# A Strassen-form feed-forward kernel: the sum S1 formed wholly by VectorE, and one small sum of product P5 queued behind an add of product P1

## The chip, the core and the metric

The kernel runs on one core of a Trainium2 chip. The metric is the device time of one execution in microseconds (us). Engines are named as in the profile: PE (TensorE matmul), PEld (its weight loads), DVE (VectorE), ACT (ScalarE), POOL (GpSimd), SP (SyncE, which here only issues DMAs).

## The reference

A causal convolution of 7 taps along the sequence, one set of softmaxed taps per head, followed by a two-layer feed-forward network with a hard-swish between the layers:

```python
# x (8, 4096, 192), weight (8, 7), w_in (192, 2048), w_out (2048, 192)
w = softmax(weight, axis=-1)
y[b, s, d] = sum_k w[head(d), k] * x_padded[b, s + k, d]     # 6 zeros ahead of each sequence
h = y.reshape(32768, 192) @ w_in
g = h * clip(h + 3, 0, 6) / 6
out = g @ w_out                                              # (32768, 192)
```

Everything is float32.

## The kernel before

**Blocks.** The 32,768 tokens go in 32 blocks of 1,024 tokens, each as two halves of N = 512. Block 0 has a path of its own. Blocks 1 to 31 each run `first_layer` and then `second_layer`. While one block is in these, DVE and ACT also form the convolution of the block after the next one.

**First layer.** The 2,048 hidden columns are 16 units of 128 x 1,024 (both token halves). A unit is 18 matmuls on PE (L438) into one of four PSUM slots, a relu on ACT (L312) and a gate multiplication on DVE (L316) that writes the result g to SBUF. A unit's slot comes free with its gate.

**Second layer.** The product g @ w_out is done in Strassen's form (Winograd's variant): g is taken as a 2 x 2 matrix of parts A11, A12, A21, A22, each of 8 chunks of 128 x 512, and seven products P1 to P7 of sums of parts replace eight. The sums needed from g are S3 = A11 - A21, S1 = A21 + A22, S2 = S1 - A11 and S4 = A12 - S2. S1 overwrites A21, S2 overwrites A11. S3 is formed towards the end of the first layer, two chunks at a time (`g_sums`, L386), three times on POOL and the last time on DVE. S1 is formed in place:

- chunks 0 to 3 by a DMA that adds (`onto`, L481, called at L513): source A22, destination A21, with `accum_op=add`, issued from POOL's queue after unit 11;
- chunks 4 to 7 by two DVE adds of 128 x 1,024 (`add`, L406, called at L515), after unit 15.

**Level two.** Output columns come in groups of 32 (q = 0, 1, 2). For the third group, products P1, P4 and P5 are themselves done in Strassen's form, with *small sums* of quarter parts of their left operand (`small_sums`, L535) and products of 128 x 256 (`small`). For P5 the operand is S1, and its small sums lie in A22's memory (`s5 = A22`): sum 1 = x21 + x22, sum 3 = x11 - x21, sum 2 = sum 1 - x11, sum 4 = x12 - sum 2. They are formed on DVE by `sum_s5`. P1's small sums are formed earlier, on POOL. P4's are gathered by adding DMAs into a tile `z` and two further tiles (L481, `z<-g` and `z<-z`), the last of them issued at L516, after the S1 adds.

**Order.** The order of the second layer is written by hand. Four streams (three column groups, and one for level two) each have a clock that counts *ticks*; a 128 x 512 matmul costs two ticks and a 128 x 256 matmul one, and the four streams use four column groups of the array at the same time. All streams end at tick 81 (45 by the assert at L691, then 2 x 8 + 2 x 2 + 2 x 8). `do(t, ...)` enters other work at t - 0.5; everything is sorted by its time and issued in that order, and each engine works through its own share in that order.

Of stream 3, the steps of `level_two(1, ...)` matter here: 4 chunks and a half of plain product until tick 9, then the small products in the order 1, 5, 6, 2, 7, 3, 4, of four ticks each. So small product 7 of P1 is at ticks 25 to 29, 3 at 29 to 33, and 4 at 33 to 37. After 7 and after 3, DVE adds a result into `p1` (L721 and L722, which the profile shows under L406 as `p<-psum,p 32x256`). These are called *add 7* and *add 3* below. Product 4 accumulates onto the same PSUM place C that add 7 reads, so PE waits at tick 33 until add 7 is done. `level_two(5, ...)` follows from tick 37: product 1 reads S1 itself, product 5 (tick 41) sum 1, product 6 (tick 45) sum 2.

The lines that put P5's small sums into this order:

```python
        for t, n in ((15.5, 1), (15.5, 3), (28.5, 2)):   # L754
            do(t, sum_s5, n)
```

Sums 1 and 3 are entered at 15.0, sum 2 at 28.0, add 7 at 28.5, add 3 at 32.5. Sum 1 overwrites a part of A22 that product P4 reads until tick 15, sum 2 one that it reads until tick 28.

Of the kernel before, what the change touches and what calls it, by code (L numbers as in the profile page):

```python
# [31 lines left out]
def kernel(  # L32
# [28 lines left out]
    NP = NC // 2  # L61
# [61 lines left out]
    def own_tiles(name):  # L123
        return [yo.tile([P, K3, N], F32, name=f"{name}{n}", tag=f"y{n}") for n in range(2)]
# [179 lines left out]
    A11, A21, A12, A22 = (g4[:, :, j] for j in range(4))  # L304
    S2, S1, S4 = A11, A21, A12
# [5 lines left out]
    def relu(r6, h):  # L311
        nc.scalar.activation(r6, h, ACT.Relu, bias=half[:], scale=1.0 / 6.0)  # L312

    def gate(g_, h):

        nc.vector.scalar_tensor_tensor(  # L316
            out=g_, in0=g_, scalar=1.0, in1=h, op0=ALU.min, op1=ALU.mult
        )
# [57 lines left out]
    def g_sums(engine, which, slots, width):  # L376

        forms = {
            3: (S3, A11, A21, ALU.subtract),
            2: (S2, S1, A11, ALU.subtract), 4: (S3, A12, S2, ALU.subtract),  # L380
        }
        for n in which:
            o, a, b, op = forms[n]
            for p in slots[::width]:
                r = slice(p, p + width)
                engine.tensor_tensor(out=o[:, r], in0=a[:, r], in1=b[:, r], op=op)  # L386
# [18 lines left out]
    def add(out, x, y, op=ALU.add):  # L405
        nc.vector.tensor_tensor(out=out, in0=x, in1=y, op=op)  # L406
# [25 lines left out]
    def products(n, slot, s, steps=range(3), begin=False, end=False):  # L432
        group, c = divmod(n, NP)
        for m_ in steps:
            wn, yn = PASSES[m_]
            for k in range(2):
                r = slice(k * D2, (k + 1) * D2)
                nc.tensor.matmul(  # L438
                    out=psum[:, 2 * slot + k], lhsT=r32(w_in_parts[wn][r, c, s]),
                    rhs=r32(y_other[r, yn, s] if group else y_own[yn][r, s]),  # L440
                    start=begin and m_ == 0, stop=end and m_ == 2, skip_group_check=True,
                )

    def places(n, slot):
        group, c = divmod(n, NP)
        return g4[:, c, 1:3] if group else g4[:, c, 0::3], psum[:, 2 * slot : 2 * slot + 2]


    def sums_a22():

        z2, z4 = (
            part[:].rearrange("p s n -> p (s n)")[:, : NP * TH // 2]
            .rearrange("p (u t) -> p u t", t=TH)
            for part in z_early
        )
        return z[:, :, 1], z2, z[:, :, 0], z4

    def first_layer(i, jobs):

        def unit(n):  # L460
            slot = free_slots.pop(0)
            for m_ in range(3):
                for s in range(K3):
                    products(n, slot, s, (m_,), s == 0, s == K3 - 1)
            to, both = places(n, slot)
            relu(to, both)
            gate(to, both)
            free_slots.append(slot)

        count = 2 * NP  # L470
        x11, x12, x21, x22 = four_parts(A22)

        def begin_sums():
            z_early[:] = own_tiles("z")
            seed(sums_a22()[1], x11, -1.0)

        def seed(to, x, sign):
            nc.scalar.mul(to, x, sign)  # L478

        def onto(to, x):  # L480
            nc.gpsimd.dma_start(out=to, in_=x, accum_op=ALU.add)  # L481


        def z13(u0, u1):
            onto(z[:, u0:u1].rearrange("p u c t -> p (u c) t"), A22[:, 2 * u0 : 2 * u1, halves[1]])

        hu = NP // 4
        s4_sums = {
            hu + 1: [lambda: seed(z[:, :hu, 0], x11[:, :hu], -1.0)],
            hu + 2: [lambda: seed(z[:, :hu, 1], x21[:, :hu], 1.0), lambda: z13(0, hu)],  # L490
            NP - 1: [lambda: seed(z[:, hu:, 0], x11[:, hu:], -1.0)],
            NP: [lambda: seed(z[:, hu:, 1], x21[:, hu:], 1.0), lambda: z13(hu, 2 * hu)],
            NP + 1: [begin_sums],
            NP + 2: [lambda: seed(sums_a22()[3], x12, -1.0)],
        }
        for job in jobs.get(-1, ()):
            job()
        for n in range(count):
            unit(n)
            for job in jobs.get(n, ()):  # L500
                job()
            for job in s4_sums.get(n, ()):
                job()
            if n == 1:
                s1.append(ot.tile([P, NP, N], F32, name="s1", tag="shared")[:])
            if n < NP and n % 2:
                small_sums(s1[-1], A11, (1, 2, 3, 4), nc.gpsimd, every[n - 1 : n + 1])
            if n > NP and n % 2:
                pair = slice(n - NP - 1, n - NP + 1)
                g_sums(nc.gpsimd if n + 1 < count else nc.vector, (3,), range(NP)[pair], 2)  # L510
                if n == NP + 3:
                    onto(sums_a22()[1], z[:, :, 1])
                    onto(S1[:, : NP // 2], A22[:, : NP // 2])  # L513
        for pair in (slice(NP - 2, NP), slice(NP - 4, NP - 2)):
            add(S1[:, pair], A21[:, pair], A22[:, pair])  # L515
        onto(sums_a22()[3], sums_a22()[1])  # L516

# [3 lines left out]
    def four_parts(x):  # L521
        return [x[:, c::2, t] for t in halves for c in range(2)]

    def small_sums(to, x, which, engine=nc.gpsimd, r=every):

        r = slice(r[0], r[-1] + 1)
        x11, x12, x21, x22 = four_parts(x[:, r])
        s1, s2, s3, s4 = four_parts(to[:, r])
        forms = {
            1: (s1, x21, x22, ALU.add), 2: (s2, s1, x11, ALU.subtract),  # L530
            3: (s3, x11, x21, ALU.subtract), 4: (s4, x12, s2, ALU.subtract),
        }
        for n in which:
            o, p, q, op = forms[n]
            engine.tensor_tensor(out=o, in0=p, in1=q, op=op)  # L535
# [13 lines left out]
    def second_layer(i, between):  # L549
        last = i + 1 == NB  # L550
        ours = [free_slots.pop(0) for _ in range(3)]
        d, e, b, c, a, x_ = (psum[:, 2 * n + k] for n in ours for k in range(2))
# [16 lines left out]
        def do(t, fn, *args, **kw):  # L569
            streams[3].append((t - 0.5, lambda: fn(*args, **kw)))  # L570
# [180 lines left out]
                s2 = four_parts(s5)[1]  # L751
                add(z[:, :, 0], four_parts(S1)[1], s2, ALU.subtract)

        for t, n in ((15.5, 1), (15.5, 3), (28.5, 2)):  # L754
            do(t, sum_s5, n)
        do(31, tiles)
        do(37, copy, out=b[m], in_=p1[:])
# [78 lines left out]
    with tc.manual_schedule():  # L836
# [101 lines left out]
        for r in range(2 * NP):  # L938
# [12 lines left out]
            n = joins.get(r)  # L951
# [72 lines left out]
        for i in range(1, NB):  # L1024
            rest = conv[2 if i > 1 else 3 :]
            jobs = {4 * n + 1: [job] for n, job in enumerate(rest[1:])}
            jobs[-1] = left + rest[:1]
            first_layer(i, jobs)
            conv = []

            def begin_conv():
                x_tiles[i + 2] = load_x(i + 2)
                conv.extend(conv_jobs(i + 2))

            between = []
            if i + 1 < NB:
                between = [(43.6, split_high), (62, split_rest), (63, swap_parts)]
            if i + 2 < NB:
                between += [(20, begin_conv), (64, lambda: conv[0]()), (72, lambda: conv[1]())]
            left = second_layer(i, between)  # L1040
# [33 lines left out]
```

## Time and profile before

| | us |
|---|---|
| median of 3 runs | 2235.2 (2234.88 to 2235.53) |
| the profiled execution | 2235.09 |
| its span in the profile | 2233.3 |
| PE busy | 2222.2 (100% of the span) |
| DVE busy | 1828.4 (82%) |
| ACT busy | 1159.6 (52%) |
| POOL busy | 893.9 (40%) |

The span is the time from the first to the last instruction that the profile records. The profiled execution's own time is 1.8 us more. Busy time of PE is modelled from pipelined matmuls, so 100% does not say that PE never paused. The granted PE clock is full in all forty slices.

### The profile page before, as it was taken

How to read it: one execution, taken by the hardware profiler on the slowest of the kernel's cores; microseconds unless marked ns; L12 is line 12 of the kernel's file. 1: busy time of each engine (PE TensorE's matmuls, PEld its weight loads, DVE VectorE, ACT ScalarE, POOL GpSimd, SP SyncE). 2: the span in 40 equal slices, each digit the busy share in tenths (PEclk: the TensorE clock that was granted, in tenths of full speed). 3: DMA queues.
4: the chain of work that ended last, by engine and by line, in shares of the span. 5: the costliest groups of instructions: out<-in, count | busy, mean ns of one | idle time of the engine just before them, and what ended most of it. 6: DMA issues, size and time to landing. Idle time of an engine off the chain costs nothing.

```text
span 2233.3 us, 51856 instructions
## 1 busy us (share of the span) xinstructions
PE 2222.2 (100%) x22466; PEld 1519.3 (68%) x22466; DVE 1828.4 (82%) x1650; ACT 1159.6 (52%) x1607; POOL 893.9 (40%) x803
## 2 busy tenths in 40 slices
PE   9999999999999999999999999999999999999998
PEld 5577767667766676766676666776677666677676
DVE  8877888878888778887888878888878888788876
ACT  7455554455554555545555445554455554555544
POOL 4534442244522445323454224542245432454423
PEclk9999999999999999999999999999999999999999
DMA  7355544545545555345553554544545545555344
GB/s 164 67 106 92 100 72 96 105 86 100 89 81 103 98 90 103 72 96 106 94 100 65 101 104 89 100 76 91 105 86 100 88 85 99 99 93 104 68 88 66
DMA packets 302180, 208.09 MB, mean 93 GB/s; under 512 B 208608, under 2 KB 261344, under 8 KB 301952
## 3 DMA queue, kind: packets, MB, share of 16 engines
q0 software_dynamic: 70320, 98.65, 27.8%
q1 hardware_dynamic: 230392, 105.86, 21.9%
q8 instruction: 176, 2.88, 0.5%
q10 hardware_dynamic: 1240, 0.27, 0.1%
q14 instruction: 52, 0.43, 0.1%
HBM read 31.72 MB, written 25.17 MB: 25 GB/s over the span
## 4 chain that ended last, share of the span: by engine, by line
PE 92%; DVE 2%; POOL 2%; DMA 2%; issue 1%; ACT 1%; SPq 0%; DVEq 0%; POOLq 0%; ACTq 0%
PE psum L573 47%; PE psum L438 44%; PE psum L327 2%; DMA g<-g 1%; POOL s L535 1%; DMA out_dram<-results 0%; DVE g L535 0%; POOL s L386 0%; DVE s L386 0%; POOL z L481 0%; DVE p L406 0%; DMA x<-in_x_dram 0%; DVE results L406 0%; SPq L353 0%; DVE g L316 0%
## 5 line engine op out<-in xcount | busy, mean ns | idle before, releaser
L573 PE MATMUL psum<-g,w_out 128*32 128x512 f32 (+1 forms) x6092 | 1055.8, 531 | 0.0
L312 ACT ACTIVATE g<-psum,half 128x1024 f32<-128x1024 f32 x512 | 570.3, 1116 | 319.7 <-PE psum L438 303.6
L535 POOL TENSOR_TENSOR s<-g 128x256 f32<-128x256 f32 x248 | 245.2, 989 | 1214.4 <-DVE g L316 928.0
L316 DVE SCALAR_TENSOR_TENSOR g<-g,psum 128x1024 f32<-128x1024 f32 x512 | 616.2, 1216 | 129.2 <-ACT g L312 128.7
L573 PE MATMUL psum<-s,w_out 128*32 128x256 f32 (+1 forms) x3272 | 631.7, 570 | 0.1
L438 PE MATMUL psum<-y,w_in 64*128 64x512 f32 x4608 | 534.9, 388 | 0.3
L438 PE MATMUL psum<-y_other,w_in 64*128 64x512 f32 x4608 | 529.0, 386 | 0.1
L438 PEld LDWEIGHTS psum<-y,w_in 64*128 64x128 f32 x4608 | 428.5, 184 | 121.5 <-issue 26.0
L573 PEld LDWEIGHTS psum<-g,w_out 128*32 128x32 f32 x6092 | 385.6, 109 | 168.6 <-issue 47.2
L438 PEld LDWEIGHTS psum<-y_other,w_in 64*128 64x128 f32 x4608 | 431.6, 184 | 91.1 <-DMA y_other<-y 0.5
L927 DVE SCALAR_TENSOR_TENSOR y<-x,c_sb,y 128x1536 f32<-128x1536 f32 x186 | 335.8, 1806 | 1.9 <-ACT y L925 1.8
L573 PE MATMUL psum<-g,w_s 128*32 128x256 f32 x1488 | 327.7, 379 | 3.2 <-DVE p L406 2.9
L386 POOL TENSOR_TENSOR s<-g 128x1024 f32<-128x1024 f32 x93 | 303.2, 3260 | 5.5 <-DVE g L316 4.8
L573 PEld LDWEIGHTS psum<-s,w_out 128*32 128x32 f32 x3272 | 223.9, 110 | 103.8 <-issue 69.3
L535 DVE TENSOR_TENSOR g<-g 128x1024 f32<-128x1024 f32 x93 | 108.7, 1220 | 152.7 <-DMA g<-g 113.3
L573 PEld LDWEIGHTS psum<-g,w_s 128*32 128x32 f32 x1488 | 154.8, 110 | 109.9 <-DVE p L406 23.4
L573 PE MATMUL psum<-z,w_s 128*32 128x256 f32 x992 | 206.3, 380 | 0.0
L386 DVE TENSOR_TENSOR s<-g 128x2048 f32<-128x2048 f32 (+1 forms) x93 | 179.9, 1934 | 1.5
L478 ACT ACTIVATE z<-g 128x512 f32<-128x512 f32 x186 | 143.0, 769 | 56.1 <-DVE g L316 54.4
L573 PE MATMUL psum<-s,w_s 128*32 128x256 f32 x744 | 170.7, 379 | 0.0
L570 ACT COPY psum<-psum 32x512 f32<-32x512 f32 (+1 forms) x217 | 106.3, 490 | 108.7 <-PE psum L573 103.9
L925 ACT ACTIVATE y<-x,c_sb 128x1536 f32<-128x1536 f32 x31 | 48.9, 1578 | 211.3 <-issue 211.3
(97 smaller groups left out, 1726.3 us busy)
## 6 DMA issues: line engine op xcount, KB each, us to landing
y_other<-y SPq DMA_DIRECT2D x124, 384.0 KB, 5.0
z<-g POOLq DMA_DIRECT2D x62, 512.0 KB, 5.4
z<-z POOLq DMA_DIRECT2D x62, 512.0 KB, 7.3
g<-g POOLq DMA_DIRECT2D x31, 1024.0 KB, 13.3
out_dram<-results SPq DMA_DIRECT2D x378, 64.0 KB, 2.0
x<-in_x_dram SPq DMA_DIRECT2D x53, 388.5 KB, 11.5
g<-in_moe_w_in_dram SPq DMA_DIRECT2D x16, 192.0 KB, 5.6
stage<-in_moe_w_out_dram SPq DMA_DIRECT2D x8, 384.0 KB, 5.2
```

The source lines that it names most:

```text
L312: nc.scalar.activation(r6, h, ACT.Relu, bias=half[:], scale=1.0 / 6.0)
L316: nc.vector.scalar_tensor_tensor(out=g_, in0=g_, scalar=1.0, in1=h, op0=ALU.min, op1=ALU.mult)
L327: lambda p=p: nc.tensor.matmul(out=bank[j * QS : (j + 1) * QS, tokens], lhsT=w_out[:, p, w, cols], rhs=x[:, p, tokens], start=(first and p ...
L386: engine.tensor_tensor(out=o[:, r], in0=a[:, r], in1=b[:, r], op=op)
L438: nc.tensor.matmul(out=psum[:, 2 * slot + k], lhsT=r32(w_in_parts[wn][r, c, s]), rhs=r32(y_other[r, yn, s] if group else y_own[yn][r, s]), ...
L478: nc.scalar.mul(to, x, sign)
L535: engine.tensor_tensor(out=o, in0=p, in1=q, op=op)
L570: streams[3].append((t - 0.5, lambda: fn(*args, **kw)))
L573: nc.tensor.matmul(out=out, lhsT=w, rhs=x, start=start, stop=True, tile_position=(0, j * QS), skip_group_check=True,)
L925: jobs = [lambda: nc.scalar.mul(y[:], x[:, :, 0:N], c_sb[:, 0:1])]
L927: jobs.append(lambda k=k: nc.vector.scalar_tensor_tensor(out=y[:], in0=x[:, :, k : k + N], scalar=c_sb[:, k : k + 1], in1=y[:], op0=ALU.mu ...
```

## The change

S1 is formed by four DVE adds of two chunks each, in the order of chunks 6-7, 4-5, 2-3, 0-1. The adding DMA for chunks 0 to 3 is gone. P5's small sum 2 is entered at 28.7 instead of 28.0, that is, behind add 7 (28.5) instead of ahead of it, and still ahead of add 3 (32.5). The order of instructions on PE, ACT and SP is the same as before; on POOL one DMA issue per block is gone; on DVE there are two more adds per block, and sum 2 and add 7 have changed places.

```diff
@@ -510,8 +510,8 @@
                 g_sums(nc.gpsimd if n + 1 < count else nc.vector, (3,), range(NP)[pair], 2)
                 if n == NP + 3:
                     onto(sums_a22()[1], z[:, :, 1])
-                    onto(S1[:, : NP // 2], A22[:, : NP // 2])
-        for pair in (slice(NP - 2, NP), slice(NP - 4, NP - 2)):
+        for c in range(NP - 2, -1, -2):
+            pair = slice(c, c + 2)
             add(S1[:, pair], A21[:, pair], A22[:, pair])
         onto(sums_a22()[3], sums_a22()[1])
 
@@ -751,7 +751,7 @@
-        for t, n in ((15.5, 1), (15.5, 3), (28.5, 2)):
+        for t, n in ((15.5, 1), (15.5, 3), (29.2, 2)):
             do(t, sum_s5, n)
```

## The prediction

> **What bounds the kernel now.** I read the page first: PE is busy for 2222.2 of 2233.3 us and the chain that ended last is 92% PE, so only time in which PE stands still can be won. The chain in order of time shows where it does (start, length, what; L438 is the first layer, L573 the second):
>
> ```profile
> 94.84 32.86 PE psum L438 x288
> 127.71 35.04 PE psum L573 x252
> 162.75 32.87 PE psum L438 x288
> ...
> 437.24 32.87 PE psum L438 x288
> 470.11 13.04 PE psum L573 x85
> 483.20 0.54 issue
> 483.81 1.16 issue
> 485.45 20.87 PE psum L573 x142
> 506.32 32.87 PE psum L438 x288
> ...
> 2124.04 35.04 PE psum L573 x255
> 2159.08 32.87 PE psum L438 x288
> ```
>
> Every first layer takes 32.9 us. The second layer takes 35.04 in blocks 1 and 30, which is 81 ticks of 0.433 us with nothing left over. In block 6 (from 470.11) it takes 36.21: the chain leaves PE at 483.2 and comes back at 485.45. From there to the end it is 20.87, so in a block of 35.04 PE gets to that place 35.04 - 20.87 = 14.17 us after its start; in block 6 at 15.34, 1.17 late. The two lists of waits say who is waited for (engine, line, releaser: total us, times, longest):
>
> ```profile
> DVE g L535 <- DMA g<-g: 113.3, 24, 5.8
> PEld psum L573 <- DVE p L406: 23.4, 28, 1.6
> ```
>
> PE waits in 28 blocks for an add into p1, and DVE ahead of that for the adding DMA of S1 (g<-g). DVE's timeline in block 6 shows the two linked (start, length, last the idle time before it):
>
> ```profile
> 473.82 2.36 DVE L406 TENSOR_TENSOR g<-g 128x1024 f32<-128x1024 f32 x2
> 481.44 3.51 DVE L535 TENSOR_TENSOR g<-g 128x1024 f32<-128x1024 f32 x3 [5.25 <-PE psum L573]
> 484.97 0.96 DVE L406 TENSOR_TENSOR p<-psum,p 32x256 f32<-32x256 f32 x2
> ```
>
> The S1 adds end at 476.18. DVE idles 5.25 us, runs sums 1, 3 and 2, then adds 7 and 3. The row names PE as releaser, but sum 1 needs of PE only ticks up to 15 (6.5 us after the start, 476.6); the DMA, issued at 467.59, is what remains, about 13.7 us to landing in this block (481.3). PE's product 4 waits for add 7, behind the three sums. Block 1 is the same work with an early DMA:
>
> ```profile
> 131.41 2.36 DVE L406 TENSOR_TENSOR g<-g 128x1024 f32<-128x1024 f32 x2
> 135.76 2.36 DVE L535 TENSOR_TENSOR g<-g 128x1024 f32<-128x1024 f32 x2 [1.99 <-DMA g<-g]
> 139.89 1.23 DVE L535 TENSOR_TENSOR g<-g 128x1024 f32<-128x1024 f32 x1 [1.77 <-PE psum L573]
> 141.15 0.43 DVE L406 TENSOR_TENSOR p<-psum,p 32x256 f32<-32x256 f32 x1
> 142.15 0.43 DVE L406 TENSOR_TENSOR p<-psum,p 32x256 f32<-32x256 f32 x1 [0.58 <-PE psum L573]
> ```
>
> Here add 7 ends at 141.58, which is 13.87 after the start 127.71 and 0.30 ahead of the 14.17 at which PE wants it: no pause.
>
> **The DMA taken out.** All the pause goes if nothing else is late at tick 33. Its size comes from the chain: the first layers of blocks 1 and 31 start at 94.84 and 2159.08, 2064.24 apart, 30 periods. A period without pause is 67.91 (94.84 to 162.75; block 30's is 67.92). 30 x 67.91 = 2037.30, so all pauses are 26.94 us. Adding up each second layer's excess over 35.04 gives 26.85, in blocks 2 to 29 alone, from 0.47 to 1.71 each. I take 26.9.
>
> POOL loses an issue of 1.79 us per block. That is worth nothing: the next POOL instruction, S3's sum of chunks 4-5, starts at 468.54 in block 6, just after the gate it needs (467.23 + 1.22 = 468.45). The other accumulating DMAs and the x loads get their megabyte of company less; no wait of PE on them is in the lists, so this counts as zero too. Were POOL's queue to hold P4's last DMA back, the cover is long: it is issued at 473.05, lands about 8.7 later (481.8), and PE reads it at tick 39, 470.11 + 16.9 = 487.0.
>
> **Two adds put in.** The row above has two adds of the same shape in 2.36 us, 1.18 each, so 2.36 per block on DVE and 73 us over 31 blocks, all in the place where DVE idled for the DMA. In times after the second layer's start (block 6): adds end at 6.07 + 2.36 = 8.43; sums 1 and 3 (2.36) end at 10.8. In block 1 add 3 starts at 14.44 after waiting for PE; add 7's product is four ticks (1.73) earlier, so add 7 can start at 12.71. DVE is therefore 1.9 us early, against 0.3 late to 1.7 late before. Bounds for an add whose price at this place no row shows: 1.18 by the rows above, and 2.41 by the same shape on POOL. At 2.41 the adds end at 10.9, the sums at 13.3, add 7 at 13.7, still ahead of 14.17. The point from which it costs PE is (14.17 - 0.43 - 2.36 - 6.07) / 2 = 2.65 per add. I take 1.18, since it is the same engine, shape and neighbours (the two adds ran beside DMAs in every block at the same 2.36). A price below zero has no source.
>
> **Sum 2 behind add 7.** Add 7 runs 12.71 to 13.14, sum 2 (1.23) 13.17 to 14.40, and add 3 starts at 14.44 as in block 1. Queued behind sum 2 on DVE are add 3 and the S2 sums; the first is not moved, by 0.04 us. If it were late by a few tenths nothing follows: the next write to what it reads is at tick 45 (19.5), which is also when PE first wants sum 2. This edit and the DMA's removal overlap: with the DMA gone, sum 2 ahead of add 7 would give block 1's 13.87, no pause either. It is worth 0 in the sum; alone, with the DMA kept, it would take up to 1.2 off each pause. It turns a margin of 0.30 into 1.03.
>
> **The sum.** The profiled execution took 2235.09 (span 2233.3 and 1.8 around it). 2235.09 - 26.9 = 2208.2. The median of the runs is 0.11 more, 2235.2: I predict 2208.3.
>
> **Rivals.**
> *Part of the pause stays.* Something besides the DMA is late at add 7, say an adding DMA that sum 3 also waits for (z<-g, whose reading of A22 must end). For it: sums wait for several semaphores, and the row in block 6 names the wrong one. Against: blocks 1, 30 and 31 have all these and no pause. If the smallest pause, 0.47, stays in 28 blocks, 13 us come back: 2221; a tenth of a us each gives 2211.
>
> *No gain: the first layer takes it back.* If DVE with 73 us more work set the pace, PE would pause in the first layer instead and the time stay near 2235. Against: in block 2, straight behind the pause-free block 1, the first layer takes 32.87 as everywhere, and everything DVE does after add 3 is timed by PE's own progress.
>
> *Slower: POOL gets ahead of the convolution.* POOL's S3 sum takes 3.9 us in block 6, 2.41 where no convolution step of DVE runs:
>
> ```profile
> 464.45 2.41 POOL L386 TENSOR_TENSOR s<-g 128x1024 f32<-128x1024 f32 x1 [0.16 <-DVE g L316]
> 467.59 1.78 POOL L481 DMA_DIRECT2D g<-g  x1
> 468.54 3.90 POOL L386 TENSOR_TENSOR s<-g 128x1024 f32<-128x1024 f32 x1
> ```
>
> DVE's convolution step (L927, two SBUF inputs) runs 468.37 to 470.18 there; 3.90 - 2.41 = 1.49 is about what of it was left when POOL began. So one of the two waits the other out, and the one that starts first wins. The removed issue stands right ahead of this POOL instruction. If POOL now started ahead of 468.37, DVE's step and the two gates behind it would come 2.4 us later, and PE, which wants the slot of gate 14 at tick 3, would pause 2.4 in 28 blocks: 2208 + 67 = 2275. Against: the POOL sum starts 0.09 after the gate it needs, and the convolution step 0.08 before that gate's end, so the order is set by the gate and not by the issue. It decides only from a shift of 0.17.
>
> The Trainium skill ("SBUF — State Buffer", "Who interferes with whom") states the same as a rule that speaks against this change: a DVE instruction with two SBUF inputs and a POOL instruction that reads SBUF exclude each other for their whole length. By that rule each new S1 add could hold up POOL, or be held up; by it alone the sum would gain up to 2.41 per block if POOL had work there. The trace agrees with the rule at L927, by the 1.49 above, and shows POOL without an SBUF-reading instruction from 472.44 in block 6 until the next block's first sums, so here it would add 0.
>
> **How the numbers follow.** Forecast 0.87 (2206.8 to 2209.8: the runs' spread of 0.3, and 0.04 per block either way, half the scatter of the first layers, which take 32.86 to 32.93); part of the pause stays 0.07; no gain 0.02; slower 0.04. The range, 2206.8 to 2212, is the forecast and the nearer part of the second case. About 0.2% (4.5 us) is what a measurement of this kernel can tell from no change. Faster takes the first two, 0.94; same 0.02; slower 0.04.
>
> **What would show it.** Right: second layers of 35.04 in all blocks, no row of PEld waiting for DVE p L406 of any size, four S1 adds of 4.7 us in a row, sums 1 and 3 straight behind them without idling, DVE idle about 1.9 us ahead of add 7. Wrong: a pause at tick 33 or a new one at ticks 3, 41 or 45, first layers above 32.9, or S1 adds well over 1.18.

## The result and the profile after

The changed kernel takes 2210.2 us (median of 4 runs, 2209.9 to 2210.5), against 2235.3 for the kernel before (median of 4). The ratio is 0.9888, 95% interval 0.9871 to 0.9905. The prediction was 2208.3, in the range 2206.8 to 2212.0. The time is in the range, the pauses went as forecast, and 1.9 us of the gain did not come.

The profiled execution took 2210.5, its span is 2208.7. The chain of the changed kernel in order of time (start, length, what), blocks 2 and 3:

```profile
162.91 32.87 PE psum L438 x288
195.78 26.47 PE psum L573 x183
...
231.60 4.07 DMA out_dram<-results
...
235.79 0.71 DVE results L412
236.50 1.70 DVE y L927
238.20 1.14 DVE g L316
...
239.39 24.78 PE psum L438 x216
264.16 35.04 PE psum L573 x256
```

and around block 6:

```profile
468.07 35.04 PE psum L573 x253
503.11 32.90 PE psum L438 x288
536.01 35.04 PE psum L573 x254
```

Every second layer of blocks 1 to 30 is now 35.04. The row of PEld waiting for DVE p L406 (23.4 us before) is gone from the list of waits. What is new is in the first piece: after block 2 the chain leaves PE, goes over a store to DRAM of 4.07 us and a DVE transpose (L412), and comes back to PE in the first layer of block 3.

DVE's timeline of block 6 (start 468.07), which answers to the one of block 6 before:

```profile
471.78 4.63 DVE L406 TENSOR_TENSOR g<-g 128x1024 f32<-128x1024 f32 x4
476.51 2.36 DVE L535 TENSOR_TENSOR g<-g 128x1024 f32<-128x1024 f32 x2
478.82 0.07 DVE L87 MEMSET x<- 64x18 f32 x1
481.20 0.43 DVE L406 TENSOR_TENSOR p<-psum,p 32x256 f32<-32x256 f32 x1 [2.31 <-PE psum L573]
481.66 1.23 DVE L535 TENSOR_TENSOR g<-g 128x1024 f32<-128x1024 f32 x1
482.92 0.96 DVE L406 TENSOR_TENSOR p<-psum,p 32x256 f32<-32x256 f32 x2
```

Four S1 adds in 4.63, sums 1 and 3 right behind, then DVE waits 2.31 for PE before add 7, which ends at 481.63, 0.6 ahead of the 482.24 (468.07 + 14.17) at which PE wants it.

The books of the two profiled spans, 2233.3 and 2208.7, 24.6 apart: pauses in second layers 26.85 before and 0.08 after (-26.8); first layers above 32.865, added up over blocks 2 to 31, 0.24 before and 1.67 after (+1.4), of it 0.47, 0.17, 0.39 and 0.41 in blocks 3, 5, 11 and 13; the stretch ahead of block 1 +0.2, the stretch from the last second layer's start to the end of the span 41.42 before and 42.00 after (+0.6). That last one is 41.2 to 41.8 in the kernels e1 to e5 and e8 below, which change little there, so I take it as scatter of single executions.

### The profile page after: what moved, and what is told of

Its sections match the earlier page's. It is cut to its first block, busy times and chain, and to the rows that moved or that the text cites. A ratio compares the mean times of both kernels' runs of the same rounds, so it can differ in the third digit from the quotient of the medians.

```text
span 2208.7 us, 51797 instructions
## 1 busy us (share of the span) xinstructions
PE 2199.7 (100%) x22466; PEld 1588.0 (72%) x22466; DVE 1898.5 (86%) x1712; ACT 1158.0 (52%) x1607; POOL 866.6 (39%) x772
## 3 DMA queue, kind: packets, MB, share of 16 engines
q1 hardware_dynamic: 230392, 105.86, 23.4%
## 4 chain that ended last, share of the span: by engine, by line
PE 96%; DVE 2%; DMA 1%; ACT 1%; SPq 0%; POOL 0%; issue 0%; DVEq 0%
PE psum L573 48%; PE psum L438 46%; PE psum L327 2%; DMA out_dram<-results 1%; DVE s L386 0%; DVE results L406 0%; SPq L353 0%; PE psum L851 0%; PE psum L859 0%; DVE y L927 0%; DVE results L412 0%; DVE y L424 0%; ACT g L312 0%; DVE g L316 0%; DMA y_other<-y 0%
## 5 line engine op out<-in xcount | busy, mean ns | idle before, releaser
L573 PE MATMUL psum<-g,w_out 128*32 128x512 f32 (+1 forms) x6092 | 1041.5, 531 | 0.0
L573 PE MATMUL psum<-s,w_out 128*32 128x256 f32 (+1 forms) x3272 | 623.9, 570 | 0.1
L573 PEld LDWEIGHTS psum<-g,w_out 128*32 128x32 f32 x6092 | 395.7, 110 | 145.3 <-issue 38.3
L573 PE MATMUL psum<-g,w_s 128*32 128x256 f32 x1488 | 316.9, 379 | 0.0
L386 POOL TENSOR_TENSOR s<-g 128x1024 f32<-128x1024 f32 x93 | 296.9, 3192 | 14.3 <-DVE g L316 13.3
L573 PEld LDWEIGHTS psum<-s,w_out 128*32 128x32 f32 x3272 | 196.8, 110 | 100.2 <-issue 78.0
L573 PE MATMUL psum<-z,w_s 128*32 128x256 f32 x992 | 201.3, 379 | 0.0
L406 DVE TENSOR_TENSOR p<-psum,p 32x256 f32<-32x256 f32 (+1 forms) x155 | 73.7, 476 | 96.5 <-PE psum L573 91.4
```

The lines of the kernel that those rows point to most:

```text
L573: nc.tensor.matmul(out=out, lhsT=w, rhs=x, start=start, stop=True, tile_position=(0, j * QS), skip_group_check=True,)
```

## The experiments

### Which half of the change carries the gain

**No DMA, old order (e1).** S1 wholly by DVE, sum 2 ahead of add 7 as before:

```diff
-        for t, n in ((15.5, 1), (15.5, 3), (29.2, 2)):
+        for t, n in ((15.5, 1), (15.5, 3), (28.5, 2)):
```

> S1 wholly by DVE as in the change, but sum 2 ahead of add 7 as before. Theory (the pause is the adding DMA's landing, and sum 2's place is worth nothing once the DMA is gone): second layers of 35.04 us in all blocks with add 7 ending some 0.3 ahead of PE, time 2210.2 within 1. Rival (sum 2 ahead of add 7 is what makes PE wait): each block keeps its smallest pause of about 0.47, 31 x 0.47 = 15, time about 2225.

Measured 2209.9 (2209.5 to 2210.2), ratio to before 0.9888 (0.9874 to 0.9903), as the changed kernel. All second layers 35.04. Its DVE timeline in block 6 (start 467.71 by the first matmul of the second layer):

```profile
479.89 1.22 DVE L535 TENSOR_TENSOR g<-g 128x1024 f32<-128x1024 f32 x1 [1.36 <-PE psum L573]
481.15 0.43 DVE L406 TENSOR_TENSOR p<-psum,p 32x256 f32<-32x256 f32 x1
```

Add 7 ends at 481.58, 13.87 after the start, as in block 1 before. The theory holds, the rival is out by 15 us: with the DMA gone, the place of sum 2 is worth nothing.

**The DMA kept, new order (e2).**

```diff
-        for t, n in ((15.5, 1), (15.5, 3), (28.5, 2)):
+        for t, n in ((15.5, 1), (15.5, 3), (29.2, 2)):
```

> The adding DMA kept, only sum 2 moved behind add 7. Theory: PE then waits for DMA landing + sums 1 and 3 (2.36) + add 7 (0.43), which is 1.2 less than before, so of the pauses of before only what exceeds some 1.2 stays, about 2.2 us over all blocks; the first layers lose what they lose in the changed kernel; time 2211 to 2213. Rival (the DMA's removal carries the gain and the order is worth nothing): 2235.

Measured 2214.0 (2213.4 to 2215.3), ratio 0.9908 (0.9891 to 0.9924). That is 1 us above what I expected, and far from the rival's 2235. Its block 2 (start 195.6) shows the rest of a pause:

```profile
199.35 2.36 DVE L406 TENSOR_TENSOR g<-g 128x1024 f32<-128x1024 f32 x2
207.40 2.36 DVE L535 TENSOR_TENSOR g<-g 128x1024 f32<-128x1024 f32 x2 [5.69 <-DMA g<-g]
209.71 0.07 DVE L87 MEMSET x<- 64x18 f32 x1
209.81 0.43 DVE L406 TENSOR_TENSOR p<-psum,p 32x256 f32<-32x256 f32 x1
```

Here the wait is put down to the DMA itself. Add 7 still comes behind it, but one sum sooner. The second layers are 3.5 us above 35.04 in all (2.2 expected; sums 1 and 3 started as late as 12.01 into the layer here, 11.93 before), the first layers 2.6. So the two halves of the change are two cures for one pause: either alone removes 23 to 27 us of the pauses at tick 33, and they do not add.

### Why the DMA was late

**x loads issued later (e4).** The kernel before, with

```diff
-                x_tiles[i + 2] = load_x(i + 2)
+                x_tiles[i + 2] = load_x(i + 2, nc.scalar)
...
-                between += [(20, begin_conv), (64, lambda: conv[0]()), (72, lambda: conv[1]())]
+                between += [(30, begin_conv), (64, lambda: conv[0]()), (72, lambda: conv[1]())]
```

> The kernel before, adding DMA and order of sum 2 kept, but the two loads of x issued from ACT's queue at tick 30 instead of from SP at the second layer's start, so that they run after the adding DMA. Theory (the DMA is late because it shares the DMA engines with the x loads; alone it lands as early as in blocks 1, 30 and 31): sums 1 and 3 start 8 to 9 us into the second layer instead of 10.7 to 11.9, no pauses, time 2209 to 2212. Rival (the DMA is late by itself, or queued behind P4's DMAs): starts stay near 11, time 2235.

Measured 2211.4 (2211.1 to 2211.6), ratio 0.9895 (0.9880 to 0.9909). Issues and times to landing, before and here (line queue, count, KB each, median us):

```profile
g<-g POOLq DMA_DIRECT2D x31, 1024.0 KB, 13.3
x<-in_x_dram SPq DMA_DIRECT2D x53, 388.5 KB, 11.5
```

```profile
g<-g POOLq DMA_DIRECT2D x31, 1024.0 KB, 11.0
x<-in_x_dram ACTq DMA_DIRECT2D x51, 388.5 KB, 5.7
```

Apart, both land sooner, by 2.3 and 5.8 us. Sums 1 and 3 start 8.1 to 10.3 us into the second layer (8 to 9 expected), and but for 0.07 us in one block there is no pause, with the adding DMA and the old order in place. The edit moves the loads to another time and to another queue at once. That the time is what counts is seen in the kernel before: blocks 1, 30 and 31, whose second layers issue no loads, have the adding DMA land 10.5, 10.5 and 11.1 us after its issue, from the same queues, against 12.8 to 14.2 in the others. And in the changed kernel, where the loads stay on SP at the old place and the adding DMA is gone, they land in 6.0 (median). So the DMA was not too slow as such: it ran into the loads of x.

### What two more adds on DVE cost

**Two and four further instructions (e5, e6).** The changed kernel with `k` = 2 or 4 maxima of an S1 pair with itself:

```diff
             add(S1[:, pair], A21[:, pair], A22[:, pair])
+            if c < 2 * k:
+                add(S1[:, pair], S1[:, pair], S1[:, pair], ALU.max)
```

> The changed kernel with two further DVE instructions of an S1 add's shape per block (the maximum of an S1 pair with itself, in place), right behind the first two chunk pairs formed. It prices the adds: the place holds as if each of the two new adds cost 2.36 us. Theory (DVE has 1.9 us or more to spare ahead of add 7, and the price from which PE waits is 2.65 per new add): sums 1 and 3 end at about 13.1 us into the second layer, add 7 still starts when PE lets it (13.2), no pause, time 2210.2 within 1. Rival (DVE has no such slack; every us more on it shows): 31 x 2.36 = 73, time 2283.

> The same with four further DVE instructions per block (4.72 us). Theory: sums 1 and 3 end at about 15.5, add 7 at 15.95, PE goes on at 16.0 instead of 14.24, a pause of 1.77 in 31 blocks, 55 us; behind the pause DVE stands 0.4 earlier against PE's end than without it, as in the kernel before, so that first layers are 32.87 again (1.5 back); time about 2264. Rival (DVE has no slack): 31 x 4.72 = 146, time 2356.

In e5 the two maxima stand behind the last two pairs formed (chunks 2-3 and 0-1) and not the first two; the work ahead of sum 1 is the same. Measured with two: 2209.4 (2209.2 to 2210.9), ratio 0.9887 (0.9872 to 0.9902), no change. With four: 2276.5 (2275.9 to 2276.9), ratio 1.0185 (1.0168 to 1.0202). Block 6 of each, two first (second layers start at 467.7 and 478.2):

```profile
471.42 7.15 DVE L406 TENSOR_TENSOR g<-g 128x1024 f32<-128x1024 f32 x6
478.68 2.36 DVE L537 TENSOR_TENSOR g<-g 128x1024 f32<-128x1024 f32 x2
480.98 0.07 DVE L87 MEMSET x<- 64x18 f32 x1
481.08 0.43 DVE L406 TENSOR_TENSOR p<-psum,p 32x256 f32<-32x256 f32 x1
```

```profile
481.88 9.67 DVE L406 TENSOR_TENSOR g<-g 128x1024 f32<-128x1024 f32 x8
491.66 2.36 DVE L537 TENSOR_TENSOR g<-g 128x1024 f32<-128x1024 f32 x2
493.96 0.07 DVE L87 MEMSET x<- 64x18 f32 x1
494.07 0.43 DVE L406 TENSOR_TENSOR p<-psum,p 32x256 f32<-32x256 f32 x1
```

With two, the S1 work is 2.52 longer and add 7 goes only 0.2 later. DVE's idle time ahead of it is used up, and add 7 ends 13.8 into the layer, 0.4 ahead of the 14.17 at which PE wants it. With four it is 5.04 longer and every second layer is 37.2, a pause of 2.19 each, 65.6 over blocks 1 to 30. I expected a pause of 1.77 and a time of about 2264. Of the 0.42 between the pauses, 0.32 is in the S1 work: 5.04 longer and not 4.72. The rival's 2283 and 2356 are out. Of the 5.04, then, 2.85 were free (5.04 less 2.19). With the 1.16 that each new add takes by itself (4.63 / 4), that is 1.16 + 2.85 / 2, some 2.6 us for each of the two, as the prediction had it and about twice their price.

### Where the missing 1.9 us went

**Four store buffers (e3).** The fourth transpose of a block writes into the buffer of its first, so it waits until that one is stored. The changed kernel with a fourth buffer:

```diff
-        xts[:] = range(3, 6)
+        xts[:] = [NP - 1, *range(3, 6)]
...
-            if last:
-                xts.insert(0, NP - 1)
```

> The changed kernel with four instead of three transposed-result buffers in every block, so that the fourth transpose of a block does not wait for the store of its first. Theory (the 1.9 us that the prediction missed are first layers of 33.0 to 33.3 in blocks 3, 5, 11 and 13, where the fourth transpose waited up to 2 us for a store and the first gate came later than about 6.87 us into the layer): all first layers 32.87, time 2208.5 to 2209.2. Rival (the two more DVE adds, or DVE's busier second layer, make the gates late): no change, 2210.2.

Measured 2208.2 (2208.0 to 2208.4), ratio to before 0.9881 (0.9866 to 0.9895): the fastest of all, 0.3 below the range that I gave and 1.7 below e1, which ran beside it and takes the time of the changed kernel. All first layers are 32.87, all second layers 35.04. The place in block 3, DVE's timeline before, after and here (the first layer starts at 231.51, 230.82 and 230.69):

```profile
235.75 0.71 DVE L412 STREAM_TRANSPOSE results<-results 96x512 f32<-96x512 f32 x1 [1.59 <-DMA out_dram<-results]
236.39 1.77 DVE L927 SCALAR_TENSOR_TENSOR y<-x,c_sb,y 128x1536 f32<-128x1536 f32 x1
238.08 2.34 DVE L316 SCALAR_TENSOR_TENSOR g<-g,psum 128x1024 f32<-128x1024 f32 x2
```

```profile
235.79 0.71 DVE L412 STREAM_TRANSPOSE results<-results 96x512 f32<-96x512 f32 x1 [1.96 <-DMA out_dram<-results]
236.43 1.77 DVE L927 SCALAR_TENSOR_TENSOR y<-x,c_sb,y 128x1536 f32<-128x1536 f32 x1
238.12 2.34 DVE L316 SCALAR_TENSOR_TENSOR g<-g,psum 128x1024 f32<-128x1024 f32 x2
```

```profile
233.73 0.71 DVE L412 STREAM_TRANSPOSE results<-results 96x512 f32<-96x512 f32 x1
234.37 1.77 DVE L925 SCALAR_TENSOR_TENSOR y<-x,c_sb,y 128x1536 f32<-128x1536 f32 x1
236.06 2.34 DVE L316 SCALAR_TENSOR_TENSOR g<-g,psum 128x1024 f32<-128x1024 f32 x2
```

The wait for the store was there before, 1.59 us, and the first gates came 6.57 into the layer with no harm (32.89). After the change they come at 7.30, and the layer is 33.34. Over the blocks, a layer is longer by what the first gate comes later than about 6.8. So the stores are one part. The other is that DVE reaches the end of a second layer 0.40 us later against PE: the second of its four transposes starts 1.24 to 1.29 us before the next first layer (its first weight load) in the changed kernel and in block 1 of the kernel before, and 1.68 us before it in the 28 blocks where the kernel before had paused at tick 33. In e6, with a pause at tick 33 in every block, it is 1.64 to 1.66 again and no first layer is above 32.89. A pause at tick 33 of 0.40 us or more hands DVE 0.40 us, and the change takes that back.

**Four store buffers, nothing else (e8).** The same edit in the kernel before.

> The kernel before with four instead of three transposed-result buffers, and nothing else. Theory (with the pause at tick 33 DVE stands 0.4 us earlier against PE's end, so the waits for the stores stay just short of delaying PE): first layers were 32.87 already, all pauses at tick 33 stay, time 2234.7 to 2235.3. Rival (the stores cost time in every kernel, and the fourth buffer is a gain of its own): 1.5 to 2 us less, 2233.3.

Measured 2230.8 (median of 11, 2230.0 to 2232.7) against 2235.6, ratio 0.9979 (0.9970 to 0.9988): neither, a gain of 4.8. The first layers are as I said, 0.22 over 32.865 in all against 0.24. The pauses at tick 33 are not: 22.6 in all, against 26.9. In the profile before, POOL's issue of the adding DMA came late in the blocks with a late store, by up to 0.7 us (1.75 us ahead of the second layer in block 13, 2.45 in block 12), 4.6 us in all; here it is 2.44 to 2.46 ahead in every block. The chain of the kernel before shows the path ahead of block 15's pause, from a store over POOL to the adding DMA:

```profile
1057.02 3.62 DMA out_dram<-results
...
1086.56 0.79 POOL z L481
1087.35 13.79 DMA g<-g
```

The ten blocks with a late issue hold the whole difference: their pauses are 11.5 in all before and 7.1 here, those of the other twenty 15.3 and 15.5. So the late stores did cost time before: they delayed POOL, POOL the adding DMA, and that lengthened the pause. My theory saw only their path over the first gates.

### The slower rival

**A POOL sum ahead of the convolution (e7).** The changed kernel with POOL's sum of chunks 2 and 3 done twice:

```diff
                 if n == NP + 3:
                     onto(sums_a22()[1], z[:, :, 1])
+                    g_sums(nc.gpsimd, (3,), range(2, 4), 2)
```

> The changed kernel with POOL's S3 sum of chunks 2 and 3 done a second time (same values), where the issue of the adding DMA stood before, so that a POOL instruction that reads SBUF is under way when DVE's convolution step behind gate 13 wants to start. Theory of the slower rival (the one that starts first makes the other wait it out, and PE wants gate 14's slot at tick 3): POOL's copy takes 2.41 and DVE's convolution step then starts, or lasts, up to 1.6 longer, gate 14 is that late, the second layers of some 28 blocks are 1 to 1.6 longer, time 2240 to 2257. Rival (only POOL is slowed, DVE never waits for it): second layers 35.04, time 2210.

Measured 2413.2 (2408.9 to 2415.6), ratio 1.0795 (1.0779 to 1.0811). Both numbers of mine were too small. POOL, then DVE, ahead of the second layer of block 6 (which begins at 494.4):

```profile
491.98 5.21 POOL L386 TENSOR_TENSOR s<-g 128x1024 f32<-128x1024 f32 x2
```

```profile
491.62 1.22 DVE L316 SCALAR_TENSOR_TENSOR g<-g,psum 128x1024 f32<-128x1024 f32 x1 [0.82 <-ACT g L312]
492.76 6.05 DVE L928 SCALAR_TENSOR_TENSOR y<-x,c_sb,y 128x1536 f32<-128x1536 f32 x1
498.74 2.34 DVE L316 SCALAR_TENSOR_TENSOR g<-g,psum 128x1024 f32<-128x1024 f32 x2
```

The convolution step, 1.81 elsewhere, takes 6.05: it gets going only when POOL is done with both its sums, at 497.19. Gate 14 is 4.2 late (498.81 less 1.81 is 497.0, against 492.76), and PE stands idle for 3.64 us in block 6 (5.60 less 1.96 in the first row below) and for 3.6 to 5.0 in each of blocks 2 to 30. The granted clock drops. By stretches (us, busy time and count by engine, last the granted clock, DMA share, GB/s):

```profile
494.40:500.00 5.60, 1.96 (x18) 0.42 (x17) 5.60 (x3) 1.66 (x2) 3.68 (x3) 0.88 0.64 106
500.00:504.00 4.00, 4.00 (x26) 1.85 (x30) 3.93 (x4) 0.34 (x1) 0.00 (x0) 0.50 0.98 207
504.00:508.00 4.00, 4.00 (x45) 2.06 (x41) 3.00 (x3) 0.90 (x2) 0.00 (x0) 0.81 0.28 53
508.00:536.00 28.00, 28.00 (x339) 20.26 (x331) 21.54 (x22) 11.62 (x22) 0.00 (x0) 1.00 0.20 43
```

At half clock in 500 to 504 another 2 us go, and some more in the next 4 us, of which the first 1.5 are at half clock too. The second layers are 204.6 above 35.04 over 29 blocks, 7.1 each. So the slower rival was real in kind. Its size is not what e7 measures: the rival had one POOL sum start ahead of the convolution step, here there are two, and no run has one alone. In the changed kernel the rival does not come: POOL, with the issue gone, idles 0.47 us for its gate, its sum before block 6 starts at 466.50, and DVE's convolution step 0.18 ahead of it, at 466.32, as read off the profile before.

## Why the prediction was right, and by what it missed

- *The time inside the range*: in part luck. The forecast itself was 2206.8 to 2209.8, and 2210.2 lies above it, in the stretch of the range that was there for a pause that stays. No pause stayed. The sign "first layers above 32.9", named as one of being wrong, came in blocks 3, 5, 11 and 13 (33.0 to 33.3).
- *What bounds, and the DMA's removal*: right. 26.9 us of pause named, 26.8 gone, and e4 shows the cause, the x loads' company.
- *Two adds*: 2.36 per block named; four adds took 4.63, so 2.27. That they are free up to twice that is shown by e5 and e6.
- *Sum 2 behind add 7, worth 0*: right by e1. A detail was off: add 7 starts 13.13 after the layer's start and not 12.71, so sum 2 ends at 14.82 and add 3 is 0.4 later than in block 1, not 0.04. The margin ahead of PE is 0.6 and not 1.03. I had counted back four ticks from add 3; its wait is for something one tick further on than the product's end, and no run says what. As the prediction said of a late add 3, nothing follows: with sum 2 in either place (e1) the next DVE add starts 15.4 into the layer.
- *The step that failed* is in the second rival, "no gain": "in block 2, straight behind the pause-free block 1, the first layer takes 32.87 as everywhere". It is true of that block, and it is one block in which the store happened to land in time (the fourth transpose waited 0.3 us there, 1.2 to 1.9 in ten of the next twenty). The same block shows DVE 0.40 late against PE (its transposes), which I did not look up. The sum had put the first layers at nothing, with 0.04 per block for scatter. The term is 1.4 us of first layers; with the scatter at both ends of the profiled execution it gives 2210.5 where I had 2208.2. Take the wait away (e3), and the time is 2208.2.
- *The slower rival* was rightly refused by the order of starts. Its price of 2.4 a block was not measured; with two POOL sums in the way (e7) it is 7.1, which includes the fall of the clock. I had not reckoned with that fall.

Why some stores land after 4 us and most after 2 is open; no run here was aimed at it. The long waits are seen mainly in first layers of odd blocks, up to block 13 in the changed kernel, 25 in e4 and 27 in e2.

## What to carry to other kernels

When one engine waits in a queue behind a transfer, look at what else is queued there and at what else moves at that time: reordering the queue, moving the other transfer or doing the work on the waiting engine are three cures of the same pause. The first and the last, made together, gained no more than the last alone (e1). Price added work against the idle time of the very stretch it goes into, and say at which price it would begin to show. When a pause goes, look again at the engine that used it to get ahead: the margin that it had in the next stage goes too, and one undisturbed block is no proof for the next thirty.

## What the hardware showed that was not expected

- A DVE instruction that waits for POOL may have to wait for more than the one POOL instruction that started ahead of it. In e7 it waited out two in a row, 5.2 us. The Trainium skill ("SBUF — State Buffer", "Who interferes with whom") has the lock held for a whole instruction by whichever started first; the trace agrees on the lock and shows that the second POOL instruction also went ahead of the waiting DVE one.
- In e6 PE stands idle for 1.2 us in every block (which makes the layer 2.2 longer), and the granted clock stays at 1.00. In e7 it stands idle for 3.6 to 5.0 us, and in most blocks the clock is at 0.50 for 6.8 us around the end of that (498.7 to 505.5 in block 6). The Trainium skill ("TensorE: Matmul & The Clock Gate", "Why this matters for your kernels") says to leave no idle gap above about 3 us, or the clock falls to half; both runs agree.
- A pause of PE at tick 33 lets DVE stand earlier against PE's end, by the pause's own length up to 0.40 us: in e2, pauses of 0.05, 0.23, 0.34 and 0.48 us move the second transpose from 1.25 us ahead of the next first layer to 1.30, 1.48, 1.59 and 1.66. Not every pause does that: in e7, with PE idle for 3.6 us or more from tick 4 on, it stands at 1.16. Why is open. That a pause lines up PE's four column streams again would be one reading; no run tests it, and e7 shows that it does not hold for a pause at any place.
